# Seven down products for one more pair, and the second half's normalisation moved

## The chip, the cores and the metric

The kernel runs on one core of a Trainium2 chip. The metric is the device time of one execution in microseconds (us), here the median of three runs.

## What is computed

The inputs are x (2048 x 512), two DFT matrices over the sequence (2048 x 2048), two over the hidden dimension (512 x 512), and the weights of a gated unit (gate and up 512 x 1792, down 1792 x 512), all float32.

```python
xn = _layernorm(x, axis=-1)
s = _A_ref(xn, ...)          # y = Re(DFT_seq(DFT_hidden(xn))) = Cr@a - Ci@b
g = _silu(_B_ref(xn, ...))   # ((sigmoid(xn @ w_gate)) * (xn @ w_up)) @ w_down
return x + s * g
```

## The kernel before, in words

Every product in float32 is made of three matmuls (`mm3`, L74 to L77): an operand is split into a high part (ScalarE copies it, L71) and a low remainder (VectorE subtracts, L72), and high x high, high x low and low x high are added up in PSUM. Large products are done as seven half-size block products instead of eight, with sums of blocks made on VectorE.

The work is a list of *units* that TensorE goes through in order (`units`, filled by `add`). Hand-written positions say what else is issued around a unit: `sooner(n, f)` puts f ahead of unit n, `after(n, f)` behind it. The operands of the next five units are loaded, and those of the next two split, before a unit runs. There is no dynamic scheduler: each engine takes its instructions in the order in which they were issued, and waits where data or a buffer is missing. All large buffers are 54 pages of 4 KB per partition in one pool. Loads are issued on SP's queue, stores on POOL's.

1. *Start* (`start`): eight tiles of 128 rows of x are normalised (`norm_a`: `bn_stats`, `bn_aggr`, and the scale by a power of -0.5 on POOL; `norm_b`: subtract and multiply on VectorE), turned by TensorE, and the first gate and up products are made.
2. *Blocks* (`block`, 13 of them in the order of `BLOCKS`; each is a half h of the rows and a pair g of 128-wide columns of the inner dimension). A block is seven units, one for each product k in the order 1, 5, 2, 6, 7, 4, 3. Each unit makes 12 matmuls for gate and up into the banks ga, ua, gb, ub, gc, uc. The product behind 6 and that behind 7 add on to the same banks `ga` and `ua`, so TensorE waits there until ScalarE's `snap` (L451) has copied them. `plus`, `gate` and `times` then form the gated values.
3. *Down products*, of the block before, run inside the units of a block. `Plain` has four items of 12 matmuls and uses the gated values as they are. `Seven` has seven items, in the order 2, 1, 6, 7, 4, 5, 3, of 6 matmuls each; it needs four sums of gated values (`sums`) and four differences of the weights (`Down.diffs`). Each item ends with `gather` (L297): two ScalarE copies out of the `pd` banks into a page, and a DMA by POOL that writes the page to `g_part[i]` in DRAM or adds it on. In `Seven`, the products 2 and 1 go to the same `g_part[i]`, so do 6 and 3, and 7 and 5. The sizes before: `Seven` for half 1 and for g of at least 3, `Plain` for the others. `SHARED` lists the pairs whose weights are prepared four units later.
4. *The second half of the rows* (tiles 8 to 15) is normalised beside the first blocks, by the table in the loop over `range(0, KH, 2)`, and stored by `store_xn`. TensorE doesn't turn these tiles: `turned_half` loads x already transposed (`x_t`), and needs mean and scale along the free dimension. So `store` writes them to `m_part` in DRAM, `both` loads them broadcast to all partitions, and four `step`s for each quarter of the rows (L187, 1024 elements each) subtract and multiply on VectorE. `x_sum(1, k)` (L246) makes the sums that the first block of half 1 needs; it starts at unit n = `turned_at` (28).
5. *Sequence products* (`seq_units`) and *hidden products* (`hidden_units`) follow; the first `ops[1, q]`, the operands of the first product, are loaded and split ahead of time.

Of the kernel before, what the change touches and what calls it, by code (L numbers as in the profile page):

```python
# [9 lines left out]
F32 = mybir.dt.float32  # L10
F32R = mybir.dt.float32r
AF = mybir.ActivationFunctionType
ALU = mybir.AluOpType
ADD, SUB = ALU.add, ALU.subtract

P = 128
# [5 lines left out]
KH = NS // NH  # L22
NT = S // 512
SB = 512
# [2 lines left out]
SCRATCH = 4096  # L27
BLOCKS = ((0, 1), (0, 2), (0, 3), (0, 4), (1, 4), (1, 5), (0, 5), (0, 6), (1, 6), (1, 0), (1, 1), (1, 2), (1, 3))
FIRST_TURNED = 1, 4
SEVEN_FROM = 3  # L30
SHARED = 4, 5, 6
SPLIT_AHEAD = 2
LOAD_AHEAD = 5

# [2 lines left out]
def fnet_glu_kernel(ctx: ExitStack, tc: tile.TileContext, x, x_t, c_re, c_im, w_h, w_gu, w_down, out):  # L37
    nc = tc.nc
    PSUM = bass.MemoryType.PSUM

    const = ctx.enter_context(tc.tile_pool(name="const", bufs=1))
    stat = ctx.enter_context(tc.tile_pool(name="stat", bufs=4))
    pages = ctx.enter_context(tc.tile_pool(name="pages", bufs=PAGES))
    dram = ctx.enter_context(tc.tile_pool(name="dram", bufs=1, space=bass.MemoryType.DRAM))
# [13 lines left out]
    nc.gpsimd.memset(mhalf, -0.5)  # L58
    warm = const.tile([P, 1], F32, name="warm")
    nc.scalar.activation(warm, mhalf, AF.Sigmoid)  # L60
    moments = const.tile([P, 2, KH], F32, name="moments")
    m_part = dram.tile([2, 2, SB], F32, name="m_part")
    xn_part = dram.tile([2, 2, 2, P, 4, D // 2], F32, name="xn_part")
    g_part = [dram.tile([P, 2, SB], F32, name=f"g_part{i}") for i in range(2 * NT)]
    gs_part = dram.tile([2 * NT, P, 2, SB], F32, name="gs_part")
# [71 lines left out]
    def after(n, f):  # L137
        extra.setdefault(n, []).append(f)

    def sooner(n, f):  # L140
        early.setdefault(n, []).append(f)


    xs = {}
# [10 lines left out]

    def norm_a(i):
        st = stat.tile([P, 6], F32, name="st")
        mv = stat.tile([P, 2], F32, name="mv")
        rs = stat.tile([P, 2], F32, name="rs")
        nc.vector.bn_stats(st, xs[i])  # L160
        nc.vector.bn_aggr(mv, st)
        mean, scale = mv[:, 0:1], rs[:, 1:2]
        if i >= KH:
            mean, scale = (moments[:, m, i - KH : i - KH + 1] for m in range(2))
            nc.gpsimd.tensor_scalar(mean, mv[:, 0:1], 0.0, None, op0=ALU.add)
        nc.gpsimd.tensor_scalar(rs[:, 0:1], mv[:, 1:2], EPS, None, op0=ALU.add)
        nc.gpsimd.tensor_tensor(scale, rs[:, 0:1], mhalf, op=ALU.pow)
        st_of[i] = mean, scale

    def norm_b(i):  # L170
        mean, scale = st_of.pop(i)
        nc.vector.tensor_scalar(xs[i], xs[i], mean, scale, op0=ALU.subtract, op1=ALU.mult)

    def turned_half(n, b, at):

        both = Load(m_part[b].rearrange("m t -> (m t)").partition_broadcast(P).rearrange("p (m t) -> p m t", m=2), [2, SB])
        raw = [Load(x_t[(2 + b) * 2 + j], [2, SB]) for j in range(2)]

        def store():
            at = slice(b * SB // P, (b + 1) * SB // P)  # L180
            for m in range(2):
                nc.gpsimd.dma_start(m_part[b, m].rearrange("(o p) -> p o", p=P), moments[:, m, at])

        def step(j, m):
            v = xraw[1, j, b] = raw[j].load()
            by = both.load()[:, m, :].unsqueeze(1).to_broadcast([P, 2, SB])
            nc.vector.tensor_tensor(v, v, by, op=(SUB, ALU.mult)[m])  # L187

        after(n, store)
        sooner(at[0] - 2, both.load)  # L190
        for i in range(4):
            if i % 2 == 0:
                sooner(at[i] - 4, raw[i // 2].load)
            after(at[i], lambda i=i: step(*divmod(i, 2)))
# [118 lines left out]
    class Plain:  # L313


        items, at = range(4), (1, 3, 4, 6)
# [70 lines left out]
    class Seven:  # L387


        items, at = SEVEN, range(7)  # L390
# [115 lines left out]
    def start(h, g):  # L506
# [48 lines left out]
        def begin():  # L555
# [7 lines left out]
            fetch(0)  # L563
            loads[0].load()
            norm_a(0)
            fetch(2, hold=True)
            loads[1].load()
# [161 lines left out]
    def seq_units(job, c_sums):  # L729
        ops = a_operands()  # L730
        left = waiting + [(job, k) for k in SEVEN]
        n = len(units)
        silu = {1: (17, 18, 20), 2: (17, 18, 20, 25, 27)}
        later = iter(range(2 * NT))
        for q in range(2):
            sooner(n - 5 + q, ops[1, q].load)
            sooner(n - 3 + q, ops[1, q].get)
        for tc_ in range(NT):
            n = len(units)
            if tc_ == 1:  # L740
# [22 lines left out]
            ps, s, made = {}, {}, {}  # L763
# [84 lines left out]
            for k in ORDER if tc_ else ORDER_FIRST:  # L848
                for pp in range(4):
                    m = len(units)  # L850
# [128 lines left out]
    with tc.manual_schedule():  # L979
        job, begin = start(0, 0)  # L980
# [3 lines left out]
        for h, g in BLOCKS:  # L984
            made = g == last
            if not made:
                w, wd, last = w_operands(g), Down(g), g
            if (h, g) == FIRST_TURNED:
                turned_at = len(units)
            job = block(h, w, made, job, Seven(h, wd, made) if h or g >= SEVEN_FROM else Plain(h, g), g in SHARED)  # L990
        for i in range(0, KH, 2):
            a, b = ((2, 9), (4, 10), (7, 12), (8, 14))[i // 2]
            if i >= 4:
                sooner(a - 4, lambda i=i: fetch(KH + i))
            for j in (i, i + 1):
                after(a, lambda j=j: norm_a(KH + j))
                after(b, lambda j=j: norm_b(KH + j))
                after(b + 1, lambda j=j: store_xn(KH + j))
        n = turned_at
        turned_half(4, 0, (n - 18, n - 17, n - 14, n - 4))  # L1000
        turned_half(8, 1, (n - 13, n - 12, n - 10, n - 3))
        for i, k in {-7: 1, -2: 2, 0: 3, 2: 4}.items():
            after(n + i, lambda k=k: x_sum(1, k))
        for i, k in {-8: 1, -5: 5, -2: 2, 0: 6, 1: 7, 3: 4}.items():
            sooner(n + i, xop[1, k].get)
# [72 lines left out]
```

## Time and profile before

| | |
|---|---|
| median of three runs | 809.51 us (809.32 to 810.89) |
| the profiled execution | 809.49 us |
| its span | 807.7 us |
| TensorE busy | 800.6 us, 3630 matmuls |
| VectorE, ScalarE, POOL busy | 639.7, 497.8, 148.6 us |
| granted TensorE clock, mean | 0.998 |
| DMA | 189.42 MB, mean 235 GB/s |

The span is what the profile covers; the time of the execution has 1.8 us more around it. Busy times are sums over an engine's instructions. A row of a timeline gives start, duration, engine, line, operation and tiles, with xN for N instructions merged; in brackets stands the idle time of the engine ahead of it and what ended that. A row of windows gives the stretch, its length, and for TensorE, weight loads, VectorE, ScalarE and POOL the busy time and the number of instructions, then the granted clock, the DMA share and GB/s. A row of waits gives who waited for whom, the total in us, how often, and the longest.

### The profile page before, as it was taken

To read this page: it belongs to the slowest core of one execution; us is meant where nothing else is said; L and a number is where in the kernel's file an instruction comes from. 1 tells how busy PE (TensorE), PEld (TensorE's weight loads), DVE (VectorE), ACT (ScalarE), POOL (GpSimd) and SP (SyncE) were. 2 spreads that over 40 slices of the span, in tenths; PEclk is the share of its full clock that TensorE was granted. 3 is DMA by queue.
4 is the path that set the end of the run, shared out by engine and by line. 5 is a ranking of instruction groups with operands and counts; after the bars stand their busy time and mean duration, and the time that the engine had idled before them with its cause. 6 is when DMAs were issued, how large, how long until landed. Compare 5 with 4: busy or idle time off the path is not lost.

```text
span 807.7 us, 10264 instructions
## 1 busy us (share of the span) xinstructions
PE 800.6 (99%) x3630; PEld 665.2 (82%) x3630; DVE 639.7 (79%) x803; ACT 497.8 (62%) x761; POOL 148.6 (18%) x218
## 2 busy tenths in 40 slices
PE   9999999999999999999999999999999999999997
PEld 7988888888888888888888888888888888888886
DVE  6897879876776778887787897888888876986945
ACT  4674657777676778778777774445445545546360
POOL 3146321221222223122111100011101210001201
PEclk9999999999999999999999999999999999999999
DMA  8366983987899998998999878278919993699976
GB/s 276 143 222 118 240 239 67 185 160 153 258 251 225 297 275 160 225 219 181 233 281 333 223 223 285 81 284 298 328 79 334 348 374 142 253 338 381 309 255 104
DMA packets 54499, 189.42 MB, mean 235 GB/s; under 512 B 6192, under 2 KB 6448, under 8 KB 54448
## 3 DMA queue, kind: packets, MB, share of 16 engines
q0 software_dynamic: 24048, 83.38, 44.5%
q1 hardware_dynamic: 30320, 105.33, 36.8%
q8 instruction: 28, 0.46, 0.2%
q14 instruction: 23, 0.19, 0.1%
q10 hardware_dynamic: 80, 0.07, 0.0%
HBM read 108.53 MB, written 83.89 MB: 238 GB/s over the span
## 4 chain that ended last, share of the span: by engine, by line
PE 98%; DMA 1%; DVE 0%; ACT 0%; SPq 0%; issue 0%
PE pd L76 7%; PE pd L77 7%; PE pd L75 7%; PE ga L75 6%; PE ga L76 6%; PE ua L76 6%; PE ua L75 6%; PE ga L77 6%; PE ua L77 6%; PE gc L76 4%; PE uc L76 3%; PE uc L75 3%; PE gc L75 3%; PE gc L77 3%; PE uc L77 3%; PE ub L76 3%
## 5 line engine op out<-in xcount | busy, mean ns | idle before, releaser
L72 DVE TENSOR_TENSOR page<-page 128x1024 fp32r<-128x1024 f32 (+1 forms) x351 | 332.5, 976 | 110.7 <-ACT page L71 110.0
L71 ACT ACTIVATE page<-page 128x1024 fp32r<-128x1024 f32 (+1 forms) x351 | 284.3, 859 | 96.0 <-DVE page L123 78.7
L123 DVE TENSOR_TENSOR page<-page 128x1024 f32<-128x1024 f32 (+2 forms) x216 | 188.8, 894 | 0.6
L301 ACT ACTIVATE page<-pd 128x512 f32<-128x512 f32 x178 | 104.8, 598 | 63.1 <-PE pd L77 48.6
L303 POOL DMA_DIRECT2D g_part<-page x81 | 71.0, 906 | 290.1 <-ACT page L301 213.0
L75 PE MATMUL pd<-page 128*128 128x512 f32 x234 | 91.0, 389 | 0.0
L76 PE MATMUL pd<-page 128*128 128x512 f32 x234 | 91.0, 389 | 0.0
L77 PE MATMUL pd<-page 128*128 128x512 f32 x234 | 91.0, 389 | 0.0
L75 PE MATMUL ga<-page 128*128 128x512 f32 x200 | 78.1, 390 | 0.0
L76 PE MATMUL ga<-page 128*128 128x512 f32 x200 | 77.8, 389 | 0.0
L75 PE MATMUL ua<-page 128*128 128x512 f32 x200 | 77.8, 389 | 0.0
L77 PE MATMUL ga<-page 128*128 128x512 f32 x200 | 77.8, 389 | 0.0
L76 PE MATMUL ua<-page 128*128 128x512 f32 x200 | 77.8, 389 | 0.0
L77 PE MATMUL ua<-page 128*128 128x512 f32 x200 | 77.8, 389 | 0.0
L75 PEld LDWEIGHTS pd<-page 128*128 128x128 f32 x234 | 43.9, 188 | 9.2
L76 PEld LDWEIGHTS pd<-page 128*128 128x128 f32 x234 | 43.9, 188 | 9.1
L77 PEld LDWEIGHTS pd<-page 128*128 128x128 f32 x234 | 43.9, 188 | 9.1
L76 PE MATMUL gc<-page 128*128 128x512 f32 x124 | 48.4, 390 | 0.0
L77 PE MATMUL gc<-page 128*128 128x512 f32 x124 | 48.3, 389 | 0.0
L75 PE MATMUL uc<-page 128*128 128x512 f32 x124 | 48.2, 389 | 0.0
L75 PE MATMUL gc<-page 128*128 128x512 f32 x124 | 48.2, 389 | 0.0
L77 PE MATMUL uc<-page 128*128 128x512 f32 x124 | 48.2, 389 | 0.0
(132 smaller groups left out, 1298.2 us busy)
## 6 DMA issues: line engine op xcount, KB each, us to landing
g_part<-page POOLq DMA_DIRECT2D x89, 512.0 KB, 7.4
page<-f_part SPq DMA_DIRECT2D x36, 512.0 KB, 5.9
page<-in_c_re_dram SPq DMA_DIRECT2D x34, 512.0 KB, 5.9
page<-in_c_im_dram SPq DMA_DIRECT2D x33, 512.0 KB, 6.4
f_part<-page POOLq DMA_DIRECT2D x28, 512.0 KB, 5.9
page<-in_w_gu_dram SPq DMA_DIRECT2D x22, 512.0 KB, 6.7
page<-xn_part SPq DMA_DIRECT2D x14, 512.0 KB, 5.5
page<-in_w_down_dram SPq DMA_DIRECT2D x11, 512.0 KB, 7.5
```

Source lines behind the costliest of these rows:

```text
L71: nc.scalar.activation(hi, src, AF.Copy)
L72: nc.vector.tensor_tensor(lo, src, hi.bitcast(F32), op=SUB)
L75: nc.tensor.matmul(ps, ws[0], ms[0], start=first, stop=False, skip_group_check=go_on)
L76: nc.tensor.matmul(ps, ws[0], ms[1], start=False, stop=False, skip_group_check=go_on)
L77: nc.tensor.matmul(ps, ws[1], ms[0], start=False, stop=last, skip_group_check=go_on)
L123: (engine or nc.vector).tensor_tensor(dst, a, b, op=op)
L301: nc.scalar.activation(pg[:, o, :], po, AF.Copy, scale=float(sign))
L303: nc.gpsimd.dma_start(g_part[i], pg, accum_op=ADD)
```

## The change

- In half 0 the pair g = 1 takes `Seven` (`SEVENS`); g = 0 is made by `start`, g = 2 stays `Plain`. `LATE` gets 1 as well, so its weights are prepared four units later.
- The tiles 8 to 15 are normalised by ScalarE (`second_norm`: `Identity` with scale and bias per partition) in place of VectorE's `norm_b`. POOL makes the bias, -mean x scale, in place of a copy of the mean. The units at which statistics and normalisation are issued move: (2, 9), (4, 10), (7, 12), (8, 14) become (1, 5), (3, 9), (6, 13), (9, 15).
- `moments` holds mean and scale of a tile side by side, and one DMA for each quarter stores them to `m_part`: 32 bytes (four tiles, two values) for each row position, where two DMAs stored single floats. After the broadcast load, `step` reads the values with a step of eight floats.
- The `step`s of `turned_half`, the second `store`, the `x_sum(1, k)` and the early loads and splits of `ops[1, q]` move to other units.

```diff
-SEVEN_FROM = 3
-SHARED = 4, 5, 6
+SEVENS = 1, 3, 4, 5, 6
+LATE = 1, 4, 5, 6
...
-    moments = const.tile([P, 2, KH], F32, name="moments")
-    m_part = dram.tile([2, 2, SB], F32, name="m_part")
+    moments = const.tile([P, KH, 2], F32, name="moments")
+    shifts = const.tile([P, KH], F32, name="shifts")
+    m_part = dram.tile([2, P, SB // P, 2], F32, name="m_part")
...
-        mv = stat.tile([P, 2], F32, name="mv")
         rs = stat.tile([P, 2], F32, name="rs")
+        mv = moments[:, i - KH, :] if i >= KH else stat.tile([P, 2], F32, name="mv")
         nc.vector.bn_stats(st, xs[i])
         nc.vector.bn_aggr(mv, st)
-        mean, scale = mv[:, 0:1], rs[:, 1:2]
-        if i >= KH:
-            mean, scale = (moments[:, m, i - KH : i - KH + 1] for m in range(2))
-            nc.gpsimd.tensor_scalar(mean, mv[:, 0:1], 0.0, None, op0=ALU.add)
+        mean, scale = mv[:, 0:1], mv[:, 1:2] if i >= KH else rs[:, 1:2]
         nc.gpsimd.tensor_scalar(rs[:, 0:1], mv[:, 1:2], EPS, None, op0=ALU.add)
         nc.gpsimd.tensor_tensor(scale, rs[:, 0:1], mhalf, op=ALU.pow)
+        if i >= KH:
+            nc.gpsimd.tensor_scalar(shifts[:, i - KH : i - KH + 1], mean, scale, -1.0, op0=ALU.mult, op1=ALU.mult)
         st_of[i] = mean, scale
+
+    def second_norm(i):
+        i_ = i - KH
+        scale, bias = moments[:, i_, 1:2], shifts[:, i_ : i_ + 1]
+        nc.scalar.activation(xs[i], xs[i], AF.Identity, scale=scale, bias=bias)
...
-        both = Load(m_part[b].rearrange("m t -> (m t)").partition_broadcast(P).rearrange("p (m t) -> p m t", m=2), [2, SB])
+        both = Load(m_part[b].rearrange("q o m -> (q o m)").partition_broadcast(P), [2 * SB])
...
-            for m in range(2):
-                nc.gpsimd.dma_start(m_part[b, m].rearrange("(o p) -> p o", p=P), moments[:, m, at])
+            nc.gpsimd.dma_start(m_part[b], moments[:, at, :])
...
-            by = both.load()[:, m, :].unsqueeze(1).to_broadcast([P, 2, SB])
+            o = SB // P
+            by = both.load().rearrange("p (q o m) -> p m o q", o=o, m=2)[:, m].unsqueeze(1).to_broadcast([P, 2, o, P])
+            v = v.rearrange("p k (o q) -> p k o q", o=o)
             nc.vector.tensor_tensor(v, v, by, op=(SUB, ALU.mult)[m])
...
-            sooner(n - 5 + q, ops[1, q].load)
-            sooner(n - 3 + q, ops[1, q].get)
+            sooner(n - 9 + 4 * q, ops[1, q].load)
+            sooner(n - 5 + 4 * q, ops[1, q].get)
...
-            job = block(h, w, made, job, Seven(h, wd, made) if h or g >= SEVEN_FROM else Plain(h, g), g in SHARED)
+            job = block(h, w, made, job, Seven(h, wd, made) if h or g in SEVENS else Plain(h, g), g in LATE)
...
-            a, b = ((2, 9), (4, 10), (7, 12), (8, 14))[i // 2]
+            a, b = ((1, 5), (3, 9), (6, 13), (9, 15))[i // 2]
...
-                after(b, lambda j=j: norm_b(KH + j))
+                after(b, lambda j=j: second_norm(KH + j))
...
-        turned_half(4, 0, (n - 18, n - 17, n - 14, n - 4))
-        turned_half(8, 1, (n - 13, n - 12, n - 10, n - 3))
-        for i, k in {-7: 1, -2: 2, 0: 3, 2: 4}.items():
+        turned_half(4, 0, (n - 16, n - 15, n - 13, n - 6))
+        turned_half(9, 1, (n - 12, n - 11, n - 10, n - 4))
+        for i, k in {-8: 1, -1: 2, 0: 3, 1: 4}.items():
             after(n + i, lambda k=k: x_sum(1, k))
```

## The prediction

> **What bounds the kernel now.** I read the page first (busy shares, then the chain that ended last), then who made TensorE wait, then TensorE's own timeline at those places.
>
> ```profile
> span 807.7 us, 10264 instructions
> PE 800.6 (99%) x3630; PEld 665.2 (82%) x3630; DVE 639.7 (79%) x803; ACT 497.8 (62%) x761; POOL 148.6 (18%) x218
> PE 98%; DMA 1%; DVE 0%; ACT 0%; SPq 0%; issue 0%
> 600.00:700.00 100.00, 100.00 (x442) 82.79 (x442) 82.03 (x75) 50.88 (x58) 11.99 (x20) 1.00 0.77 280
> PEld ga L75 <- ACT page L454: 0.8, 2, 0.5
> ```
>
> TensorE is the chain: 98% of it. In the stretch from 600 to 700 us, where only 512-wide matmuls run, 442 of them fill 100 us, so one costs 100/442 = 0.226 us. After the start-up there is nearly no idle time to win: the waits list has just two waits of TensorE's weight loads, 0.8 us together, both on a ScalarE copy that frees the bank `ga` (L454, `snap`). So the change can gain by removing matmuls or these two waits, and can lose by any new wait. Here are the two places, TensorE first:
>
> ```profile
> 168.93 0.39 PE L77 MATMUL pd<-page 128*128 128x512 f32 x1
> 169.28 0.50 PE L75 MATMUL ga<-page 128*128 128x512 f32 x1
> 169.62 0.40 PE L76 MATMUL ga<-page 128*128 128x512 f32 x1
> ...
> 401.79 0.39 PE L77 MATMUL pd<-page 128*128 128x512 f32 x1
> 402.20 0.50 PE L75 MATMUL ga<-page 128*128 128x512 f32 x1
> 402.54 0.40 PE L76 MATMUL ga<-page 128*128 128x512 f32 x1
> ```
>
> Start to start should be 0.226. At 169 it is 0.35 and 0.34, so 0.23 is lost. At 402 it is 0.41 and 0.34, so 0.29 is lost. In both, about 0.11 is the slow restart behind the wait.
>
> **Part 1: seven down products for g = 1 of half 0.** `Plain` issues 4 items x 2 banks x 2 halves of the pair x 3 = 48 matmuls, `Seven` 7 x 2 x 3 = 42. Six fewer, 6 x 0.226 = 1.36 us, all on the path: **-1.36**. What it adds lies beside TensorE: three more gathers (two copies each), three more splits, the split of `dif`, four small differences and four sums. The rows for their prices, and for the stretch in which they fall:
>
> ```profile
> L301 ACT ACTIVATE page<-pd 128x512 f32<-128x512 f32 x178 | 104.8, 598 | 63.1 <-PE pd L77 48.6
> L71 ACT ACTIVATE page<-page 128x512 fp32r<-128x512 f32 x161 | 95.9, 627 | 25.3 <-DVE page L123 17.1 <-DVE page L472 6.1 <-DVE page L547 1.5
> L172 DVE TENSOR_SCALAR page<-page,moments 128x512 f32<-128x512 f32 x8 | 4.0, 543 | 0.0
> 38.00:98.00 60.00, 59.99 (x266) 49.33 (x265) 48.14 (x78) 36.80 (x64) 27.96 (x47) 1.00 0.73 179
> ```
>
> ScalarE gets about 6 x 0.6 + 3 x 0.63 + 1.1 = 6.6 us more, and in part 2 eight normalisations more (5.0 at the 0.63 of a 512-wide operation): 11.6 us. In these 60 us it is busy 36.8, so 23 idle hide it on average. VectorE gets some 7 us (at its 0.69 for 512 elements, rows below) and loses 8 x 0.54 = 4.3, with 11.9 us idle. Cost on the path: **0**, if the cover holds in each unit. The tightest place is the `snap` of unit 10, which now has the two normalisations put after unit 9 ahead of it:
>
> ```profile
> 78.30 0.60 ACT L454 ACTIVATE page<-ga 128x512 f32<-128x512 f32 x1 [1.60 <-PE ga L77]
> ```
>
> Before, ScalarE stood idle 1.60 us for TensorE here. Now it has a gather's two copies, a gate, two normalisations and two splits ahead of the `snap` within that unit; following its queue with the prices above I find some 0.2 us of cover left. Below, I price the case that it is gone.
>
> **Part 2: normalising on ScalarE.** No trace row shows `Identity` with two per-partition operands. Nearest rows: 0.60 (from PSUM), 0.63 (from SBUF); I take 0.63, as its operand lies in SBUF, and 1.05, twice as wide a split (1.59 - 0.54 in the row at 167.16 below), as a high bound. Twice 0.42 more, less the 0.2 of cover, would cost about 0.7 at unit 10, and perhaps 0.3 again at the other pairs. Nothing excludes that it is cheaper, but cheaper is worth nothing: it is hidden. `store_xn` on POOL now waits for ScalarE; the gathers queued behind it only free pages, with the limit worked out in the third rival.
>
> **Part 3: `m_part` in 32-byte pieces.** Each store now writes 128 pieces and not two times 512 of 4 bytes; two issues on POOL go.
>
> ```profile
> g_part<-page POOLq DMA_DIRECT2D x3, 512.0 KB, 3.0
> ...
> m_part<-moments POOLq DMA_DIRECT2D x2, 2.0 KB, 11.2
> ...
> g_part<-page POOLq DMA_DIRECT2D x4, 512.0 KB, 11.9
> ...
> g_part<-page POOLq DMA_DIRECT2D x20, 512.0 KB, 5.1
> ...
> SPq L86 <- DMA m_part<-moments: 38.4, 2, 23.4
> ```
>
> These are the DMA issues of 40 to 60 us (first), 74 to 98 (second and third) and 112 to 200 us (fourth): 2 KB take 11.2 us, as long as the 512 KB gathers issued around them, which need 3.0 (plain) or 5.1 (accumulating) elsewhere; and SP's queue stands 38.4 us behind the two. That goes, but nothing on TensorE waits for it now: **0**. It is the cover for the three more accumulating gathers; see the rivals. The price sits on VectorE: the eight steps of `turned_half` now read mean and scale with a step of eight floats. No row shows such a read. The nearest is the same step read densely:
>
> ```profile
> L187 DVE TENSOR_TENSOR page<-page 128x1024 f32<-128x1024 f32 x8 | 9.8, 1221 | 0.0
> 98.00:140.00 42.00, 42.00 (x187) 34.79 (x186) 35.65 (x54) 27.40 (x48) 7.05 (x9) 1.00 0.67 171
> ```
>
> I take the 1.22 unchanged, because at 1024 elements in 1.22 us VectorE already goes at about one element per ns; bounds are 1.22 and, as a doubling, 2.4. VectorE's idle time from 98 to 140 is 6.4 us, so up to half as long again (8 x 0.6 = 4.9) is hidden.
>
> **Part 4: the moved steps around the first turned block** (its first unit, n, begins near 153 us: four units of 18 matmuls, 4.08 us each, ahead of the wait at 169). `x_sum(1, 2)` goes from after unit n-2 to after n-1, `x_sum(1, 4)` from after n+2 to after n+1. This is what sets the wait at 169, so I follow it. VectorE and ScalarE before:
>
> ```profile
> 154.23 0.68 DVE L464 TENSOR_TENSOR page<-page,gc 128x512 f32<-128x512 f32 x1
> 154.82 0.68 DVE L464 TENSOR_TENSOR page<-page,uc 128x512 f32<-128x512 f32 x1
> 155.61 0.69 DVE L472 TENSOR_TENSOR page<-page 128x512 f32<-128x512 f32 x1
> ...
> 161.03 2.96 DVE L72 TENSOR_TENSOR page<-page 128x1024 fp32r<-128x1024 f32 x3 [0.53 <-ACT page L71]
> 163.91 0.69 DVE L123 TENSOR_TENSOR page<-page 128x512 f32<-128x512 f32 x1
> 165.91 1.22 DVE L246 TENSOR_TENSOR page<-page 128x1024 f32<-128x1024 f32 x1
> 167.04 0.69 DVE L123 TENSOR_TENSOR page<-page 128x512 f32<-128x512 f32 x1
> ...
> 164.63 0.63 ACT L71 ACTIVATE page<-page 128x512 fp32r<-128x512 f32 x1 [1.19 <-DVE page L123]
> 165.17 1.07 ACT L301 ACTIVATE page<-pd 128x512 f32<-128x512 f32 x2
> 166.13 0.60 ACT L469 ACTIVATE page<-gb 128x512 f32<-128x512 f32 x1
> 167.16 1.59 ACT L71 ACTIVATE page<-page 128x1024 fp32r<-128x1024 f32 x2 [0.43 <-DVE page L246]
> 168.65 0.57 ACT L454 ACTIVATE page<-ga 128x512 f32<-128x512 f32 x1
> ```
>
> An `x_sum` (L246) takes 167.04 - 165.91 = 1.13 start to start. In the new program order `x_sum(1, 4)` stands right ahead of the total at 163.91, for which ScalarE's split at 164.63 waits. So, in the times of before: total 165.04, split 165.76, the two gather copies and the gate 1.13 later, so the gate at 167.26. A copy from PSUM takes (166.13 - 165.17) / 2 = 0.48 start to start, so ScalarE is free at 167.74. The two splits then needn't wait (their `x_sum` is long done): 167.74 + (168.65 - 167.16) = 169.23 for the `snap`, against 168.65: **0.58 later**.
>
> `x_sum(1, 2)` now stands between the additions of `plus` (154.23, 154.82) and the product at 155.61. Without it, `plus` could come up to 1.13 earlier; the `lo` operation ahead of it waits for its split, so I take 0.7. Then the product starts at 154.82 + 0.59 - 0.70 + 1.13 = 155.84, **0.23 late**, and the chain behind it (through the split that VectorE waits for at 161.03) has no slack up to 163.91. Bounds: 0 (`plus` a full 1.13 earlier) and 0.93 (not earlier at all). Both engines' queues hang on TensorE's own earlier units, so the 1.36 of part 1 shifts all of this alike. The wait of 0.23 at 169 grows by 0.58 + 0.23 to 1.04: **+0.81**, bounds 0.58 and 1.51.
>
> **Part 5: the early splits of `ops[1, q]`.** ScalarE ahead of the wait at 402:
>
> ```profile
> 393.42 1.23 ACT L301 ACTIVATE page<-pd 128x512 f32<-128x512 f32 x2 [1.81 <-issue]
> ...
> 398.63 3.04 ACT L71 ACTIVATE page<-page 128x1024 fp32r<-128x1024 f32 x4
> 401.57 0.59 ACT L454 ACTIVATE page<-ga 128x512 f32<-128x512 f32 x1
> ```
>
> Of the four splits at 398.63, one is that of `ops[1, 0]`, 1024 wide. A 512-wide split takes 165.17 - 164.63 = 0.54 start to start, so the 1024-wide one in the pair at 167.16 takes 1.49 - 0.54 = 0.95. It goes two units up, where ScalarE idles (1.81 at 393 alone). The `snap` comes 0.95 earlier, TensorE lost 0.18 plus the restart, so the wait goes: **-0.29**; next late is the same `snap`, with 0.7 us to spare. Its two loads go four units and one unit up in SP's queue and hold two pages longer; no TensorE wait in the list hangs on a load.
>
> **Sum:** -1.36 + 0.81 - 0.29 = -0.84. The profiled run took 809.49 (span 807.7 and 1.8 around it), 0.02 from the median of 809.51: **808.7 us**, 0.1% faster, which is inside the 0.2% (1.6 us) that a measurement of this kernel can tell from no change.
>
> **Rivals.**
>
> *The added wait doesn't appear.* If VectorE's order at 163 costs nothing, -1.36 - 0.29 = -1.65, or -1.88 if the old 0.23 goes too: 807.6 to 807.8, just over 0.2%. For it: the 1.19 us idle of ScalarE ahead of 164.63. Against: that idle is the very wait for the total that moves. 0.13.
>
> *Strided reads.* If a step of eight floats halved the rate, each step would take some 1.13 us more, 9.0 in all against 6.4 idle. The two late steps (units n-6 and n-4) put 2.3 us more into two units, 8.2 us, in which 15% idle (6.4 of 42) give 1.2: 1.1 late, or 1.4 in the order of the queue, where the last step stands ahead of sums that ScalarE splits. I take 1.4, near 140 us: 810.1, no change. Beyond, each further 0.1 us per step costs about 0.3, as three steps then come late in a row, so it is slower by 0.2% only from some 1.45 us more per step. [...] 0.17, of it 0.05 beyond the 0.2%.
>
> *Accumulating gathers land late (slower).* Products 2 and 1 of `Seven` both add to `g_part[0]`, so the second waits in POOL's queue for the first to land, and what POOL has queued behind it (`norm_a`'s steps, `m_part`, `xn_part`) waits too.
>
> ```profile
> 75.07 0.97 POOL L303 DMA_DIRECT2D g_part<-page  x1 [1.46 <-ACT page L301]
> ```
>
> That is the first accumulating gather; with 6 matmuls less ahead of it and ScalarE's copies sooner it comes near 73 us. The second's page goes to a split in unit 13, which must start by about 94, as a gather copy behind it frees the `pd` bank that TensorE needs near 95: the rival decides when a landing takes over (94 - 73.4) / 2 = 10.3 us. At the 11.9 of the row, 2 x 1.6 = 3.2 late, plus about 1 at the next bank: 808.7 + 4 = 812.7. For: just that row. Against: it holds where the `m_part` stores fill the queue and SP's held-up loads come in a burst; at 112 to 200 us it is 5.1. 0.12.
>
> *ScalarE's normalisation is dear* (1.05): +1.0, 809.7. 0.05.
>
> **Numbers.** Forecast 0.53, at 808.5 to 809.4 by the bounds of part 4. Faster 0.13; slower 0.12 + 0.05 = 0.17; same 0.53 + 0.12 + 0.05 = 0.70. The range of 807.6 to 811.5 leaves out most of the late landings and of the far end of strided reads.
>
> **What would show it.** 3624 matmuls; the wait at 402 gone; one wait on `ga` near 168 of about 1 us, and no other over 0.3 between 40 and 800; `m_part` landing within 5 us; steps of `turned_half` at 1.2 us; `Identity` at 0.6. Wrong: steps at 2 us and more, a wait on `pd` near 95, or none on `ga` at 168.

## The result: slower, by a steady half microsecond and a varying rest

The changed kernel takes 812.0 us (median of 22 executions, 809.93 to 814.77) against 809.62 for the kernel before on the same chip: ratio 1.0022, interval 1.0012 to 1.0031. The forecast was 808.7. The two fastest executions differ by less, 809.93 against 809.20, so two things are to be explained: a steady loss that every execution has, and one that varies. The page and TensorE's stalls below are of an execution near the fastest (810.45 us, span 808.7), where nearly only the steady loss is to be seen.

```profile
span 808.7 us, 10264 instructions
PE 800.0 (99%) x3624; PEld 664.4 (82%) x3624; DVE 649.7 (80%) x807; ACT 507.4 (63%) x779; POOL 153.5 (19%) x219
PE 93%; DVE 4%; issue 1%; ACT 1%; POOL 0%; DVEq 0%; ACTq 0%
```

The six matmuls are gone. In the chain that ended last TensorE's share falls from 98% to 93%; VectorE has 4%. The timeline of TensorE shows where:

```profile
80.82 0.39 PE L78 MATMUL pd<-page 128*128 128x512 f32 x1
81.23 0.50 PE L76 MATMUL ga<-page 128*128 128x512 f32 x1
...
139.64 0.39 PE L78 MATMUL pd<-page 128*128 128x512 f32 x1
140.81 0.50 PE L76 MATMUL ga<-page 128*128 128x512 f32 x1 [0.78 <-ACT page L460]
141.15 0.39 PE L77 MATMUL ga<-page 128*128 128x512 f32 x1
...
169.30 0.39 PE L78 MATMUL pd<-page 128*128 128x512 f32 x1
170.49 0.50 PE L76 MATMUL ga<-page 128*128 128x512 f32 x1 [0.81 <-ACT page L460]
```

Start to start should be 0.226. At 140 it is 1.17 and then 0.34: 0.94 + 0.11 = 1.05 lost. At 169 it is 1.19: 0.96 + 0.11 = 1.08 (0.23 before). At 81 it is 0.41: 0.18 + 0.11 = 0.29 (none before). All three wait on `ga` for `snap` (L460 now). The wait at 402 is gone. The sum is -1.36 - 0.29 + 1.05 + 0.85 + 0.29 = **+0.54 us**, against 0.73 between the fastest executions. The spans of the two profiled executions differ by 1.0; most of the rest is their start-up, as the first wait behind it, which both kernels have, comes at 38.99 us and not at 38.70.

The groups that have a new price, and then `m_part` and the gathers in the DMA issues of 74 to 98 us:

```profile
L193 DVE TENSOR_TENSOR page<-page 128x1024 f32<-128x1024 f32 x8 | 17.3, 2162 | 0.0
L173 ACT ACTIVATE page<-page,shifts,moments 128x512 f32<-128x512 f32 x8 | 6.1, 809 | 0.0
```

```profile
g_part<-page POOLq DMA_DIRECT2D x5, 512.0 KB, 6.2
...
m_part<-moments POOLq DMA_DIRECT2D x1, 4.0 KB, 2.5
```

A step that reads mean and scale eight floats apart takes 2.16 us in place of 1.22. `Identity` takes 0.81. The store of `m_part` lands after 2.5 us in place of 11.2 (8.0 in place of 10.4 in the stretch of 40 to 74 us), and the gathers around it after 6.2 in place of 11.9. VectorE and ScalarE ahead of the wait at 140, from the timeline:

```profile
133.89 2.17 DVE L193 TENSOR_TENSOR page<-page 128x1024 f32<-128x1024 f32 x1
135.97 0.70 DVE L124 TENSOR_TENSOR page<-page 128x512 f32<-128x512 f32 x1
136.57 2.44 DVE L73 TENSOR_TENSOR page<-page 128x1024 fp32r<-128x1024 f32 x3
138.91 1.30 DVE L124 TENSOR_TENSOR page<-page 128x512 f32<-128x512 f32 x2
...
139.65 0.63 ACT L72 ACTIVATE page<-page 128x512 fp32r<-128x512 f32 x1 [0.27 <-DVE page L124]
140.18 0.58 ACT L460 ACTIVATE page<-ga 128x512 f32<-128x512 f32 x1
```

VectorE has no idle time here: the step pushes back the sums behind it, ScalarE's split waits for one of them, and the `snap` that frees `ga` stands behind the split.

### The profile page after: what moved, and what is told of

Same layout as the page of the kernel before. It is cut to its first block, busy times and chain, and to the rows that moved or that the text cites. A ratio compares the mean times of both kernels' runs of the same rounds, so it can differ in the third digit from the quotient of the medians.

```text
span 808.7 us, 10264 instructions
## 1 busy us (share of the span) xinstructions
PE 800.0 (99%) x3624; PEld 664.4 (82%) x3624; DVE 649.7 (80%) x807; ACT 507.4 (63%) x779; POOL 153.5 (19%) x219
## 3 DMA queue, kind: packets, MB, share of 16 engines
HBM read 108.53 MB, written 85.47 MB: 240 GB/s over the span
## 4 chain that ended last, share of the span: by engine, by line
PE 93%; DVE 4%; issue 1%; ACT 1%; POOL 0%; DVEq 0%; ACTq 0%
PE pd L78 6%; PE pd L77 6%; PE pd L76 6%; PE ga L76 5%; PE ga L77 5%; PE ga L78 5%; PE ua L77 5%; PE ua L78 5%; PE ua L76 5%; PE ub L76 3%; PE ub L78 3%; PE ub L77 3%; PE gc L77 3%; PE gb L76 3%; PE gb L78 3%; PE uc L77 3%
## 5 line engine op out<-in xcount | busy, mean ns | idle before, releaser
L72 ACT ACTIVATE page<-page 128x1024 fp32r<-128x1024 f32 (+1 forms) x355 | 287.6, 857 | 100.9 <-DVE page L124 82.2
L124 DVE TENSOR_TENSOR page<-page 128x1024 f32<-128x1024 f32 (+2 forms) x224 | 192.8, 880 | 0.7
L307 ACT ACTIVATE page<-pd 128x512 f32<-128x512 f32 x184 | 107.2, 598 | 51.0 <-PE pd L78 40.0
L309 POOL DMA_DIRECT2D g_part<-page x84 | 74.4, 935 | 288.4 <-ACT page L307 158.8
L77 PE MATMUL gc<-page 128*128 128x512 f32 x124 | 48.4, 390 | 0.0
L78 PE MATMUL gc<-page 128*128 128x512 f32 x124 | 48.2, 389 | 0.0
L76 PE MATMUL uc<-page 128*128 128x512 f32 x124 | 48.2, 389 | 0.0
L77 PE MATMUL uc<-page 128*128 128x512 f32 x124 | 48.2, 389 | 0.0
L78 PE MATMUL uc<-page 128*128 128x512 f32 x124 | 48.2, 389 | 0.0
```

The source lines that it names most:

```text
L72: nc.scalar.activation(hi, src, AF.Copy)
L76: nc.tensor.matmul(ps, ws[0], ms[0], start=first, stop=False, skip_group_check=go_on)
L77: nc.tensor.matmul(ps, ws[0], ms[1], start=False, stop=False, skip_group_check=go_on)
L78: nc.tensor.matmul(ps, ws[1], ms[0], start=False, stop=last, skip_group_check=go_on)
L124: (engine or nc.vector).tensor_tensor(dst, a, b, op=op)
L307: nc.scalar.activation(pg[:, o, :], po, AF.Copy, scale=float(sign))
```

## The experiments

Theory: three steady waits, each from one part of the change, and a varying loss from transfers that land late and hold pages. Rivals: another place for the steady loss, or a loss by the gathers of the new `Seven`. Each time stands beside the kernel before on the same chip, as the median of that kernel goes from 809.54 to 810.74 between these runs.

**The changed kernel once more.**

> The changed kernel once more, to see a second execution. The times so far spread from 809.9 to 814.8 where the kernel before stays within 809.2 to 810.6, and the profiled one was near the low end (810.45). Theory A (gather landings near 205 to 230 us hold pages that ScalarE wants; late in part of the executions): median near 812, and in a profile of an execution over 811.5 a wait of 1 to 3 us on pd or ga between 220 and 232, with gathers landing after 8 us or more there. Theory B (the three more accumulating gathers of the new Seven job land late): the lost time stands between 73 and 105 us, on pd near 95. In both the four waits known from the first profile (0.3 at 39, 0.3 at 81, 1.05 at 140, 1.08 at 169) stay.

812.55 us (12 executions, 809.99 to 813.69), before 810.74; ratio 1.0011 (0.9992 to 1.0029). Its profile is again of a short execution (810.09), with the same three stalls, to 0.02 us. So the waits are steady, and what moves the median by 2 us does not show in them. Between the theories A and B of the varying loss this short execution decides nothing.

**Mean and scale stored as before.**

```diff
-            nc.gpsimd.dma_start(m_part[b], moments[:, at, :])
+            for m in range(2):
+                nc.gpsimd.dma_start(m_part[b, m].rearrange("(o p) -> p o", p=P), moments[:, m, at])
...
+            by = both.load()[:, m, :].unsqueeze(1).to_broadcast([P, 2, SB])
```

> The changed kernel with mean and scale stored and read as before (two stores of single floats for each quarter, dense reads). Theory (strided reads cost 0.94 us each and make the wait at 140): steps back at 1.22 us, the wait at 140 gone, fastest executions 1.0 us under those of the changed kernel (809.9 to 808.9). Rival (strided reads are hidden, the wait at 140 has another cause): same time, wait stays. The two stores per quarter land after 10 us again; if theory B holds, gathers at 73 to 100 land later and the kernel loses 2 us or more near 95.

818.19 us (five executions, 817.26 to 819.75), ratio 1.0095 (1.0081 to 1.0109): slower by 6 us than the changed kernel. The wait at 140 is gone, as the steps read densely again, but the timeline shows a new one on `pd` (then the window of 106 to 109 us), and the DMA issues of 74 to 98 us its reason:

```profile
104.87 1.09 ACT L309 ACTIVATE page<-pd 128x512 f32<-128x512 f32 x2 [6.59 <-DMA g_part<-page]
...
105.52 0.80 PE L76 MATMUL pd<-page 128*128 128x512 f32 x1 [5.32 <-ACT page L309]
106.11 0.63 PE L77 MATMUL pd<-page 128*128 128x512 f32 x1
```

```profile
106.00:109.00 3.00, 3.00 (x8) 2.32 (x8) 2.45 (x4) 1.55 (x3) 0.00 (x0) 0.50 1.04 270
```

```profile
g_part<-page POOLq DMA_DIRECT2D x5, 512.0 KB, 14.3
...
m_part<-moments POOLq DMA_DIRECT2D x2, 2.0 KB, 10.9
```

ScalarE's gather copy waits 6.59 us for a page that an earlier gather holds. After 5.32 us of idle time TensorE's matmuls start 0.43 apart and not 0.226, for 12 of them, at a granted clock of 0.50 (the third number from the end of the window's row). What lowers the clock there is not shown. So "gathers land late" is real, and the new form of the store (one in place of two, in 32-byte pieces; the run does not separate these) keeps it away.

**The sums of x at the four units of before.**

```diff
-        for i, k in {-8: 1, -1: 2, 0: 3, 1: 4}.items():
+        for i, k in {-7: 1, -2: 2, 0: 3, 2: 4}.items():
```

> The changed kernel with the four x_sum(1, k) at the units of before. Theory (x_sum(1, 4) ahead of the total, and x_sum(1, 2) behind plus, make the wait at 169 1.08 instead of 0.23): wait at 169 back to about 0.2, wait at 140 1.05 to 1.3, together 0.7 us faster. Rival (the wait at 169 comes from the strided reads or from the eight normalisations): wait at 169 stays at 1.0.

810.21 us (809.35 to 812.52), ratio 0.9993 (0.9982 to 1.0005). In the timeline the place at 169 is as in the kernel before, 0.33 and 0.34 start to start, 0.22 lost:

```profile
169.81 0.39 PE L78 MATMUL pd<-page 128*128 128x512 f32 x1
170.14 0.50 PE L76 MATMUL ga<-page 128*128 128x512 f32 x1
170.48 0.39 PE L77 MATMUL ga<-page 128*128 128x512 f32 x1
```

Part 4 of the prediction holds, cause and price. The trace of the changed kernel shows its chain too: the `x_sum` at 164.54 us stands right ahead of the total at 165.68, for which ScalarE is idle 2.33 us. The other two waits stay; the one near 140 costs 1.25 here, not 1.05.

**`Plain` for pair 1.**

> The changed kernel with Plain for g = 1 (48 matmuls instead of 42, three gathers less). Theory A: fastest executions 1.1 us slower (1.36 more for six matmuls, 0.3 less as the wait at 81 goes), spread of 3 us and more stays, median near 813. Theory B: the spread goes with the three gathers, all executions within 1 us, median near 811, faster than the changed kernel.

811.63 us (810.77 to 815.85), ratio 1.0020 (1.0007 to 1.0034). The wait at 81 is gone, those at 140 and 169 stay. Its profile caught a longer execution (812.34), with a wait that no short one has:

```profile
317.97 0.39 PE L78 MATMUL pd<-page 128*128 128x512 f32 x1
319.34 0.50 PE L76 MATMUL ga<-page 128*128 128x512 f32 x1 [0.98 <-ACT page L460]
```

There ScalarE's split waits 1.79 us for a page that a gather holds, and the `snap` stands behind it. So the varying loss can come without the new `Seven`, and far behind its place. But the median is 0.87 over the fastest here, against 2.56 in the changed kernel on the same chip: that the new `Seven` adds to the loss is not ruled out.

**Seven products alone**, on the kernel before:

```diff
+SEVENS = 1, 3, 4, 5, 6
+SHARED = 1, 4, 5, 6
...
+            job = block(h, w, made, job, Seven(h, wd, made) if h or g in SEVENS else Plain(h, g), g in SHARED)
```

> The kernel before with one edit: pair 1 of half 0 makes its down products as seven, its weights prepared four units later; everything else (VectorE's normalisation, the two stores of single floats, positions) as before. Prediction's part 1: six matmuls fewer are worth 1.36 us, and nothing is lost beside them: 3624 matmuls, 808.2 us for a kernel that took 809.5. Rival (tight place near 80 us): the snap of unit 10 stands behind the earlier copies and splits on ScalarE, and the wait on ga there grows to about 1.2 us, so the gain is gone: 809.4, no change. Late landings would show as a wait on pd near 95 to 100 us of some microseconds, and then 812 or more.

816.9 us (six executions, 813.0 to 819.95), ratio 1.0074 (1.0050 to 1.0098). Both rivals at once, as the timeline of an execution of 813.08 us shows:

```profile
82.04 0.50 PE L75 MATMUL ga<-page 128*128 128x512 f32 x1 [1.16 <-ACT page L454]
99.03 0.50 PE L75 MATMUL pd<-page 128*128 128x512 f32 x1 [1.70 <-ACT page L301]
104.47 0.50 PE L75 MATMUL pd<-page 128*128 128x512 f32 x1 [1.07 <-ACT page L301]
```

Part 1 by itself loses. Within the changed kernel it pays: its fastest execution is 0.78 us below that of the run with `Plain` on the same chip (809.99 against 810.77).

**Thin stores of the sequence differences**, in the changed kernel and then in the kernel before. `s_part` is written near 220 to 235 and 275 to 295 us. Both kernels leave that part of the output out.

```diff
-                nc.gpsimd.dma_start(to, v)
+                thin = 1 if make is diffs and ahead == 3 else 4
+                nc.gpsimd.dma_start(to[:, 0:thin, :], v[:, 0:thin, :])
...
-            v1, v3, v2, v4 = (Load(s_part[q, i], [4, D // 2]) for i in range(4))
+            v1, v3, v2, v4 = (Load(xn_part[q, i % 2, i // 2], [4, D // 2]) for i in range(4))
```

> The changed kernel, but the eight stores of the first sequence product's block differences (s_part, near 220 to 235 and 275 to 295 us) write a quarter of their columns, and the loads that read them read blocks of xn_part of the same size instead; that part of the output is left out. Compute, queues and positions stay. Theory A: what the changed kernel loses in most executions beside its steady waits (its median is 2 us above its fastest) comes from gathers and s_part stores that land late in the stretch of 200 to 320 us and hold pages, so with three quarters of those stores' bytes gone the s_part landings near 278 us fall from 12 to 13 us to under 8, and the median comes down to within 0.5 us of the fastest, about 810.2. Rival B: the loss comes from elsewhere (the stretch of 70 to 180 us, or the end); the median stays at 811.5 to 812.6.

> The kernel before, with the edit of the run thin_s alone: the eight s_part stores write a quarter of their columns and the loads that read them read blocks of xn_part; that part of the output is left out. If the varying loss is the same mechanism in both kernels, the median of this one comes to its fastest too, 809.2 to 809.5, and between the two kernels with thin stores only the steady waits are left: 810.2 for the changed kernel in thin_s less this, 0.6 to 0.9 us. Rival (only the changed kernel is open to late landings): this one's median stays as far above its fastest as that of the kernel before on the same chip.

810.19 us (809.98 to 811.47) and 809.55 (809.40 to 810.21), on two chips where the kernel before takes 810.07 and 809.67. The spread is nearly gone in both (the one long execution of 811.47, which the profile caught, still waits 0.66 and 0.49 us near 226 and 228), and the medians differ by 0.64 us, near the 0.54 of the steady waits. The windows of 240 to 300 us, of the changed kernel and then of its thin version (the last three columns are clock, DMA share, GB/s):

```profile
240.00:270.00 30.00, 30.00 (x134) 24.82 (x133) 19.65 (x33) 21.71 (x39) 5.96 (x7) 1.00 1.04 239
270.00:300.00 30.00, 30.00 (x134) 24.85 (x133) 23.00 (x32) 21.74 (x38) 8.21 (x11) 1.00 1.05 303
```

```profile
240.00:270.00 30.00, 30.00 (x134) 24.86 (x133) 19.66 (x33) 21.64 (x39) 5.93 (x7) 1.00 0.97 225
270.00:300.00 30.00, 30.00 (x134) 24.86 (x133) 23.01 (x32) 21.18 (x37) 8.21 (x11) 1.00 0.97 262
```

TensorE is full in both. The DMA share is 1.04 and 1.05 in the first and 0.97 in the second; that this is the room which a late transfer needs is a reading, not shown.

**Mean and scale spread out once by ScalarE.**

```diff
+            src = both.load().rearrange("p (q o m) -> p m o q", o=o, m=2)
+            nc.scalar.activation(pg.rearrange("p m (o q) -> p m o q", o=o), src, AF.Copy)
...
+            by = dense.get()[:, m, :].unsqueeze(1).to_broadcast([P, 2, SB])
```

> The changed kernel, but for each half of the second rows ScalarE copies the broadcast mean and scale once into a page in which each lies densely (it reads with the step of eight floats), and the eight steps on VectorE read that page. Theory (strided reads cost 0.94 us for each step and make the wait of 1.05 us near 140 us): the steps fall to 1.2 us, the wait near 140 goes, those near 81 and 169 stay; 1.05 us less than the changed kernel, fastest 808.9. Rival (the wait near 140 comes from the moved positions, not from the price of the steps): the steps get shorter and the wait stays.

811.5 us (809.45 to 813.90), ratio 1.0015. The wait at 140 is gone and the other two stay, as expected. The fastest of 12 executions, on another chip, gained only 0.5 of the 1.05, in part because a new wait of TensorE on `pd` near 100 us costs 0.39. Every later run has the dense page and this wait (0.27 to 0.40), while the changed kernel has none there. The groups (`step` is L199 here, the copy L187):

```profile
L199 DVE TENSOR_TENSOR page<-page 128x1024 f32<-128x1024 f32 x8 | 9.8, 1221 | 2.6 <-ACT page L187 2.6
L187 ACT ACTIVATE page<-page 128x1024 f32<-128x1024 f32 x2 | 4.4, 2179 | 0.0
```

The strided read costs ScalarE as much (2.18 us), but two such reads do for eight steps.

The profile is of a long execution. It loses 1.50 us on `ga` at 403.7, behind 2.44 us in which ScalarE waits for a page that a gather holds, and 2.68 us at 433, 437 and 442. There ScalarE waits for loads:

```profile
434.77 1.06 ACT L72 ACTIVATE page<-page 128x1024 fp32r<-128x1024 f32 x1 [2.73 <-DMA page<-in_c_re_dram]
```

So the varying loss has a second form: not only gathers but also loads for the sequence products come late.

**All three steady waits repaired**: the dense page, the sums of x as before, and the second pair of tiles normalised after unit 8. It was run twice, and once with thin stores.

```diff
-            a, b = ((1, 5), (3, 9), (6, 13), (9, 15))[i // 2]
+            a, b = ((1, 5), (3, 8), (6, 13), (9, 15))[i // 2]
```

> The dense page as in the run named dense, and also the sums of x at the four units of the kernel before, and the second pair of tiles normalised by ScalarE after unit 8 in place of 9. If the three steady waits (0.29 near 81, 1.05 near 140, 0.85 near 169 us) are all that the changed kernel loses in an undisturbed execution, then all three go, and what is left is the gain of six matmuls and of the wait at 402: fastest 807.7 to 808.0, 1.5 us under the kernel before's fastest of 809.2; no wait on ga over 0.3 us between 40 and 330 us. Rival: an edit brings a new wait in the place of an old one, and the fastest stays above 808.6.

> The run dense_x8 once more, beside spread on the same chip: fastest 808.1, median 810 to 811, waits on ga or pd of some microseconds near 226, 318 or 402 us if its profile falls on a long execution.

> The run dense_x8 with thin s_part stores (that part of the output is left out). If the steady waits and the varying loss add up to all that the change costs, both are gone here: fastest 807.9 to 808.1, median within 0.5 us of it, 1.2 us under thin_before. Rival: a further loss is in the change that neither edit touches; the median stays over 808.8.

The fastest are 808.08 and 808.01, against 807.7 to 808.0 worked out. The three waits are gone; a wait near 100 us, which came with the dense page, is new:

```profile
99.80 0.39 PE L78 MATMUL uc<-page 128*128 128x512 f32 x1
100.19 0.50 PE L76 MATMUL pd<-page 128*128 128x512 f32 x1
```

Start to start is 0.39, so 0.16 + 0.11 is lost, about 0.28. With it the steady account closes to 0.2 us on the second run's chip and to 0.4 on the first's. The medians are 810.65 and 810.20 (before 810.07 and 809.67; ratios 1.0001, 0.9983 to 1.0018, and 0.9985, 0.9967 to 1.0002). With thin stores the median is 808.24 (807.99 to 809.42), 1.31 under the thin version of before. The second run's profile, of 811.20 us, shows the varying loss:

```profile
225.28 1.09 ACT L313 ACTIVATE page<-pd 128x512 f32<-128x512 f32 x2 [4.21 <-DMA g_part<-page]
...
224.14 0.39 PE L78 MATMUL ua<-page 128*128 128x512 f32 x1
225.93 0.50 PE L76 MATMUL pd<-page 128*128 128x512 f32 x1 [1.40 <-ACT page L313]
```

ScalarE waits 4.21 us for a page that a gather holds, TensorE 1.40 for ScalarE: the chain of the run with the old stores, 120 us later. In the short execution of the same kernel (808.35) this copy waits 1.27 us for the same gather and TensorE does not wait: what varies is the landing.

**The first four sums, with their stores, moved apart.**

```diff
-        sums_ahead(diffs, xn_blocks(0), s_part[0], (n + 15, n + 16, n + 17, n + 18), 3)
+        sums_ahead(diffs, xn_blocks(0), s_part[0], (n + 15, n + 17, n + 19, n + 21), 3)
```

> The run dense_x8, with the four sums and stores of the first sequence product's block differences that stand at four units in a row (15, 16, 17, 18 behind unit 28) two units apart instead (15, 17, 19, 21). If late landings near 226 us make most of the varying loss, there is about 1 us more room there: the fastest stays at 808.1, and the median comes down from 2.6 us above the fastest to 1.0 to 1.5, 809.1 to 809.6. Rival: the loss moves to the next places (318, 402 us), and the median stays 2 us or more above the fastest.

812.61 us (809.02 to 814.42), ratio 1.0017 (0.9997 to 1.0036). Refuted: the median went up by 2.4 against the run beside it, and even the fastest by 1.0. Its profile, of 809.97 us, has waits at 372 and 438 in place of 226, as the rival said; at 438 ScalarE had waited 1.86 us for a load of `s_part`. The edit moves VectorE's sums too, so it tests more than the stores.

**Fewer gathers, with the whole output.** Products 2 and 1 of `Seven` go to the same `g_part`. Their two pages are added on chip and gathered once, where the first would accumulate: by VectorE one item later, or by POOL at once.

```diff
+        if k in (2, 1):
+            kept.append(pg)
+            return
+        if kept:
+            a, b = kept
+            kept.clear()
+            combine(a, a, b, ADD)
+            send(i_first[0], a)
```

> The run dense_x8, but where product 2 of Seven would add on to g_part, its page is kept; VectorE adds product 1's page to it one item later, and one gather takes both: 11 accumulating gathers of 512 KB fewer, each worth two page transfers in DRAM, and two pages held about 4 us longer. Theory (the amount of DMA work between 200 and 320 us makes landings late): fastest 808.0 to 808.9, median within 1 us of it, DMA share of 240 to 300 us under 1.00 where it was 1.05. Rival (held pages decide): a steady wait on pd, gc or ga near 212 us of 0.9 us or more, and a median 2 us or more above 808.1.

> The same, but POOL adds the two pages as soon as product 1 is copied, ahead of its gather in POOL's own queue. What POOL takes for 1024 elements no trace of this case shows. Theory (amount of DMA work): as merge_late, fastest 808.0 to 808.5, if POOL's addition takes under 3 us. Rival: POOL's addition is so long, or slows VectorE's work beside it so much, that gathers behind it land later and the median is above 811.

With VectorE: 809.81 us (809.20 to 811.76), ratio 0.9999 (0.9987 to 1.0010). The median is 0.6 over the fastest, where it was 2.6, but the fastest is 1.1 above that of the repaired kernel: its trace has one new wait, for a split on VectorE. So neither the theory nor the rival came out whole.

```profile
443.47 0.39 PE L76 MATMUL gc<-page 128*128 128x512 f32 x1
444.65 0.50 PE L77 MATMUL gc<-page 128*128 128x512 f32 x1 [0.79 <-DVE page L73]
```

With POOL: 813.15 us, ratio 1.0027 (1.0013 to 1.0042). Its fastest, 811.66, is 3.6 above 808.08: waits of 0.95 and 2.03 us on `ga` come back at 82 and 172. The group of POOL's sums, and from the timeline one of them with a sum of VectorE beside it:

```profile
L124 POOL TENSOR_TENSOR page<-page 128x1024 f32<-128x1024 f32 x11 | 29.8, 2712 | 72.7 <-ACT page L315 72.7
...
166.73 3.07 POOL L124 TENSOR_TENSOR page<-page 128x1024 f32<-128x1024 f32 x1 [6.16 <-ACT page L315]
...
167.45 2.90 DVE L124 TENSOR_TENSOR page<-page 128x512 f32<-128x512 f32 x1
```

POOL's sum takes 2.71 us on average. While one runs, VectorE's 512-wide sum takes 2.90 us, where such a sum takes 0.69 elsewhere; ScalarE's split waits 1.80 us for it, and the `snap` stands behind the split. At 79 us two such sums take 2.60, where they take 1.26 in the version in which VectorE adds. So POOL's sum slows VectorE beside it. VectorE's 512-wide splits grow only from 0.69 to 0.75 on average, and that average hides it.

**Ten merges in place of eleven**, the last `Seven` gathering as before.

```diff
-                i_first[0] = i_ if i_ in begun else None
+                i_first[0] = i_ if i_ in begun and i_first[1] < 10 else None
+                i_first[1] += i_first[0] is not None
```

> merge_late with ten merges: the last Seven of the list, whose pages would be added near 415 to 440 us, gathers products 2 and 1 one by one as before. If VectorE's added sum is what makes the split at 443 us late, the wait on gc there goes and the fastest comes to 808.0 to 808.4, the median to 808.3 to 808.9, 1 us or more under the kernel before on the same chip. Rival (landings make that wait): it stays at 0.7 us or more, fastest 808.9 to 809.2.

**808.19 us** (12 executions, 807.89 to 808.94) against 809.54 on that chip: ratio 0.9975, interval 0.9961 to 0.9989. It beats both kernels, the kernel before by 0.25%. The wait at 443 is gone, so the last merge made it; in the run with eleven merges, ScalarE waits 1.12 and 0.73 us for VectorE's sums just ahead of it. Its page, and then its windows:

```profile
span 806.3 us, 10242 instructions
PE 98%; DVE 1%; POOL 0%; issue 0%; ACT 0%
```

```profile
240.00:270.00 30.00, 30.00 (x134) 24.82 (x134) 21.51 (x35) 21.64 (x40) 5.18 (x6) 1.00 0.91 216
270.00:300.00 30.00, 30.00 (x134) 24.86 (x133) 24.18 (x33) 21.78 (x38) 7.42 (x10) 1.00 1.04 304
```

From 240 to 270 the DMA share falls from 1.05 in the repaired kernel to 0.91; from 270 to 300 it stays 1.04, and the kernel still does not lose. So not every full stretch costs time; that the room ahead of it is enough is argued, not shown. The repaired kernel was not run on this chip. The profile counts 80.22 MB written to DRAM, where the repaired kernel writes 85.47, and 108.53 MB read in both: of the two transfers that each merge was expected to save it shows one. In time an accumulating gather is nearer two: from 112 to 200 us of the changed kernel, where POOL's queue carries gathers alone, they take 69.4% of the 16 engines' time for 10.70 MB, and the loads 7.1% for 2.10 MB, so a MB gathered takes 1.9 times as long as a MB loaded.

## Why the prediction was wrong, step by step

- **Part 1, -1.36 and hidden**: the six matmuls are right. "Cost on the path: 0" is wrong by 0.29, at the place that the text named, unit 10. That cost needs parts 1 and 2 together: `Plain` takes the wait away, and in the repaired kernel so does normalising one unit earlier.
- **Part 2, 0.63 for `Identity`**: it is 0.81, between the taken value and the high bound of 1.05. Twice 0.18 more, less the cover of 0.2, is 0.16 late, and the restart adds 0.11: the 0.29 above, as near as the estimated cover allows. The text priced this at 0.7 at the far bound; a size missed, the mechanism right.
- **Part 3, "I take the 1.22 unchanged"**: this step failed in the steady account. The steps take 2.16, inside the bounds of 1.22 and 2.4, and the near end was taken because VectorE "already goes at about one element per ns"; that says nothing of an operand with a stride. The eight steps take 7.5 us more, against 6.4 idle on VectorE and the 4.9 that the text held to be hidden. The halved rate by which the rival priced them was a supposition: no row of before shows a strided step, and the runs show 0.94 us more for each (2.16 in the changed kernel, 1.22 in the run dense) where it took 1.13. Why a strided step takes longer no run shows. The rival's chain and place (near 140) were right; of its two prices, 1.1 and 1.4, it took the far one, and 1.05 was lost. That its time of 810.1 is within 0.4 of the profiled execution is luck: its 1.4 equals three mis-sized terms together, of which it knew one.
- **Part 4, +0.81**: right. The wait on `ga` at 169 costs 1.08 where 1.04 was worked out, and putting the four sums back takes it away.
- **Part 5, -0.29**: the wait at 402 is gone in short executions; in a long one (the run dense, profiled at 813.90) a late page brings it back, with 1.50 us.
- **The sum**: -0.84 + 1.05 + 0.29 + 0.04 = +0.54 for undisturbed executions. So 1.4 of the 3.3 us between 808.7 and 812.0 are the terms that were mis-sized. The rest, 1.9 us, is no term of the sum.
- **Late gathers**: ruled nearly out near 95 us, rightly: there they land after 6.2 us, as the small stores are gone. That this rival's time, 812.7, is near the 812.0 measured is luck, as its place was wrong. The failing step is "at 112 to 200 us it is 5.1": the text looked no further than 200, and put what comes later at nothing. The same gather copy on ScalarE in the profiled executions of before, changed and ten merges, all short:

```profile
222.01 1.28 ACT L301 ACTIVATE page<-pd 128x512 f32<-128x512 f32 x2 [1.35 <-PE pd L77]
```

```profile
225.07 1.09 ACT L307 ACTIVATE page<-pd 128x512 f32<-128x512 f32 x2 [2.91 <-DMA g_part<-page]
```

```profile
220.98 1.28 ACT L322 ACTIVATE page<-pd 128x512 f32<-128x512 f32 x2 [1.55 <-PE pd L78]
```

  Before the change and with ten merges it waits for TensorE's product alone. In the changed kernel it waits 2.91 us for a page that a gather holds, and TensorE is not yet held up; in the two executions in which it waits 3.54 (changed, thin stores) and 4.21 (repaired) TensorE loses 0.77 and 1.67 at its next product. Waits of 3.10 (repaired, thin stores) and 3.22 (eleven merges) cost at most 0.1. The median landing of the gathers of 205 to 260 us does not tell these apart: 6.1 before, 7.7 changed and 7.0 with ten merges, but 8.1 with eleven.

  DMA was full there before the change too, as the windows of the kernel before show (share 1.02 and 1.04), and its profiled execution, a short one, still has no stall there.

```profile
240.00:270.00 30.00, 30.00 (x134) 24.85 (x133) 20.22 (x33) 21.73 (x40) 6.85 (x8) 1.00 1.02 246
270.00:300.00 30.00, 30.00 (x134) 24.83 (x133) 23.07 (x32) 21.79 (x38) 7.39 (x10) 1.00 1.04 294
```

  The prediction took one profiled execution for all, and its range held no loss by an execution that differs.
- **Open**: that the varying loss comes from late transfers is shown for the changed and the repaired kernel, by the stalls in their long executions and by thin stores and merged gathers, which take it away. For the kernel before the thin stores alone show it. How it is shared between late gathers and late loads is not shown; nor is why the changed kernel has it more often. What makes its gathers land later was not found, and moving the sums and stores apart made it worse. The x sums alone at their old units also narrowed the spread (median 0.86 over the fastest, against 2.56), as `Plain` did, while the repaired kernel, which has the x sums there too, shows 2.6 and 2.2; 12 executions don't settle that.

## What to carry to other kernels

Don't price a strided operand by the dense row of the same instruction: here a step of 32 bytes cost 77% more. If eight instructions read it, spread it out once on an engine that has room, and look for the new wait that this copy makes. Before saying that a page comes back in time, look at the DMA share of every later stretch, and at the waits of ScalarE and not only of TensorE: here the profile of a short execution showed 2.91 us of waiting that cost nothing, while half of the executions took 2 us or more above the fastest. In this kernel fewer transfers cured that, and the one try of moving them did not.

## What was not expected of the hardware

- A VectorE `tensor_tensor` in float32 of 1024 elements takes 2162 ns with one operand at a step of 32 bytes, 1221 densely; a ScalarE copy with the same step 2179.
- ScalarE's `Identity` with scale and bias for each partition takes 809 ns for 512 elements, where a split of the same width takes 627.
- Beside two stores of 2 KB in single floats the 512 KB gathers take 14.3 us to landing from 74 to 98 us, against 6.2 beside one store of 4 KB in 32-byte pieces.
- POOL's float32 sum of two 1024-wide pages takes 2.71 us, and a 512-wide float32 sum of VectorE beside one takes 2.90 in place of 0.69.
